# A gated recurrence and a squared-ReLU layer pair: the second token group's second layer wholly in three passes, with six weight differences summed in DRAM by GpSimd's DMAs

## The chip, the cores and the metric

The kernel runs on one core of a Trainium2 chip. The metric is the device time of one execution in microseconds (us). Three runs of the kernel before gave 520.93, 521.38 and 521.76 us; the median is 521.38. One more execution was taken by the hardware profiler and took 521.61 us.

The engines are called as in the profile: PE (TensorE, matrix products), PEld (its weight loads), DVE (VectorE), ACT (ScalarE), POOL (GpSimd) and SP (SyncE, which issues most DMAs). Each engine works through its own instructions in program order and waits on semaphores for the others.

## The reference

```python
def _attn_ref(q, k, v, alpha):          # each (4, 8, 768, 48)
    state = np.zeros((B, H, D, D), dtype=np.float32)
    for t in range(S):
        state = alpha[:, :, t, :, None] * state + np.einsum('bhd,bhe->bhde', k[:, :, t], v[:, :, t])
        y[:, :, t] = np.einsum('bhd,bhde->bhe', q[:, :, t], state)
...
def _moe_ref(x, w_in, w_out):           # x (3072, 384), w_in (384, 2048), w_out (2048, 384)
    h = np.maximum(x @ w_in, 0.0)
    return (h * h @ w_out).astype(np.float32)
```

The recurrence's output, turned to 3072 rows of 384, is x. The weights come in 64-bit floats, which the kernel turns into 32-bit ones itself.

## The kernel before

**Groups and layers.** The sequence is cut in chunks of 128 steps; there are 24 blocks (4 batches by 6 chunks), taken in groups of four: six groups of 512 rows of x. For each group PE does the first layer (16 tiles "h" of 128 hidden units by 512 rows) and the second layer (four sums "o" of 128 rows by 384). While a group's layers run, the recurrence of later blocks is woven in, two blocks at a time ("attention"): its sums of logarithms "cs", transposes "T", scores and state sums "sckv", and products "y".

**Two forms of product.** The weights are held in 8 pieces each (two hidden tiles per piece). A plain product in 32-bit floats shows as two PE records. A product in three passes splits both factors into a near part and a rest, in a faster 32-bit form: near by near, rest by rest, and a third pass with the differences of the two. For the weights the parts are wb (near), wl (rest) and wd (difference); for x they are xa, xl, xd; for the hidden tiles ha, hl, hd (some of the ha and hl lie in other buffers, "hx").

- Group 0: first layer plain; second layer six pieces plain, the last two (6 and 7) in three passes (`k0` = 2).
- Group 1: first layer in three passes; second layer pieces 0 to 3 plain, 4 to 7 in three passes (`k1` = 4).
- Groups 2 to 5: both layers in three passes.

**Making the weights' parts.** `prepare` plans four steps per piece: `cast_w` (ACT, L665, makes wb), `rest_w` (DVE through `combine`, L660, makes wl), `scale_w` (ACT, L679, scales wl, then `keep` stores it to DRAM, L670) and `diff_w` (DVE, L660, makes wd and stores it). wb stays on the chip; wl and wd are loaded again for each group by `pump` (L703), in the order of the list `todo`, as slots come free.

**Splitting the hidden tiles.** `split_h` (ACT, L710, makes ha; DVE, L660, makes hl) and `diff_h` (DVE, L714, makes hd) come once per hidden tile that takes part in three passes. In group 1 before there are 8 such tiles.

**The second layer.** `out_plain` issues plain products and takes the sum out on ACT (L843). `out_x` issues the first two passes tile by tile, and joins the plain part on DVE (L857) or, where there is none, takes the sum out on ACT (L861). `out_y` issues the third passes, piece pairs for each of the four sums, adds on DVE (L660, "osb") and stores. All its products are at L820, those of the first layer in three passes at L737.

**The order of work.** `weave` runs a list of PE units with estimated costs and inserts events (attention steps, weight preparation, splits of x) at planned times, counted in these costs; the planned times stand in the table `AT`. Nothing is reordered afterwards: each engine's order is the order of the calls. `sp` (DVE, L287 and L288) makes "hi" and "lo" of the logarithms for the matmuls of `cs` (L300, L301). `bl` and `br` take one row through DRAM by SP's DMAs (L334, L344, "last<-row") for DVE's `next_state` (L490). In `ga` a marker on GpSimd (L529) waits for PE, and PE's products of `gb` wait for that marker. `align` (L1018) inserts NOPs into PE's instructions at the places and pads of `AT`.

Of the kernel before, what the change touches and what calls it, by code (L numbers as in the profile page):

```python
# [18 lines left out]
AT = {'v_by': (2.5, 3.5, 5.0), 'before': 2.2, 'places': ((4, 203), (16, 188)), 'pads': ((1, 33.0, 218), (2, 0.5, 83), (2, 5.5, 178)), 'evs': 0.65, 'lead': 4, 'post': 3, 'w_first': (45.25, 42.0, 55.95), 'wstep': 1.6, 'w_in_at': 2.5, 'w_late': 0.6, 'w_in_by': 3.4, 'room1': 22, 'room': 25, 's0': 4, 'ahead': 6, 'late': 2, 'xs': 0.2, 'g0': ((1.5, 4, False, True, 28.25), (20.25, 6, True, True), (28.75, 8, True, False)), 'sc0': (2.35, 2.35, 2.35), 'g1': ((5.5, 8, False, 15.5), (15.5, 10, True), (34.5, 12, True)), 'g': ((1.7, 6, True), (15.5, 8, True)), 'g1x': 50.0, 'gx': 48.25, 'g0x': 55.25, 'k0': 2, 'h0': 16, 'k1': 4, 'h1': 3, 'h1by': 2, 'evs0': 0.3, 'tp': 'ADMD', 'tp1': 'ADAD', 'split': 8, 'o0': (44.75, 47.25), 'o1': (), 'o2': (21.75, 27.5, 31.75, 35.0, 41.25, 41.75), 'str1': 22.0, 'ga': 9.5, 'gb': 13.0, 'cv0': 1.5, 'first': 'ln0 warm0 cs0 load0v load2a ei0 load1v eb0 mk0 ln1 fill1 fill1 kT0 cs1 kc0 eb1 mq0 qT0 mq1 ei1 qc0 fill1 mk1 fill1 lt0 sc0 lt1 kT1 kv0 qT1 am0 ln2 weights2 us0 load2q kc1 qc1 cs2 sc1 fill1 am1 load2k ei2 load3a eb2 load4a fill1 kv1 st0 first0 us1 fill1 middle0 ln3 mq2 load3k ya0 qT2 yb0 mk2 fill1 qc2 kT2 cs3 kc2 load3q load2v weights5 sc2 eb3 load3v fill1 sga0 sgb0 fill1 ei3 ev0 mq3 mk3 am2 fill1 late0 qT3 kT3 sgc0 first1 kc3 qc3 middle1 kv2 ha0 sc3 us2 kv3 sga1 ha1 am3 us3 sgb1 load4k ya2 load4q load4v first2 yb2 late0 sgc1 middle2 weights6 ev2 lt3 lt2 st2 ha3 ha2 sgb2 sga2 hb1 sgc2 hb0 hb2 weights1 st1 hb3 st3 weights0'}  # L19
# [6 lines left out]
def kernel(  # L26
# [634 lines left out]

    def cast_w(w, p):
        need(("w", p + (NW if w == "o" else 0)))
        b = here["b", w, p] = wt("wb", FP32R, shapes[w])
        nc.scalar.activation(out=b, in_=whole[w][p], func=AF.Copy, scale=NEAR)  # L665
# [3 lines left out]
    def keep(x, w, p):  # L669
        nc.sync.dma_start(out=kept_parts[x, w, p], in_=words(made[x, w, p]))  # L670
        stored.add((x, w, p))

    def rest_w(w, p):
        l = made["l", w, p] = wt("wl", FP32R, shapes[w])
        combine(((l, whole[w][p], ALU.subtract, here["b", w, p].bitcast(FP32)),))

    def scale_w(w, p):
        l = made["l", w, p]
        nc.scalar.activation(out=l, in_=l.bitcast(FP32), func=AF.Copy, scale=1.0 / E)  # L679
        keep("l", w, p)  # L680

    def diff_w(w, p):
        b, l = here["b", w, p].bitcast(FP32), made["l", w, p].bitcast(FP32)
        d = made["d", w, p] = wt("wd", FP32R, shapes[w])
        cut.add((w, p))
        combine(((d, b, ALU.subtract, l),))
        keep("d", w, p)
        for x in "ld":
            t = made.pop((x, w, p))
            if w == "i" or p >= NW - AT["k0"] or (x == "l" and p >= NW - AT["k1"]):  # L690
                here[x, w, p] = t
        pump()

    def prepare(at, w, p, late=0):
        step = AT["wstep"]
        fs = (cast_w, rest_w, scale_w, diff_w)
        return [(at + i * step + late * (i > 1), f, (w, p)) for i, f in enumerate(fs)]
# [11 lines left out]
    def split_to(a, l, x):  # L709
        nc.scalar.activation(out=a, in_=x, func=AF.Copy, scale=NEAR)  # L710
        combine(((l, x, ALU.subtract, a.bitcast(FP32)),))

    def diff_to(d, a, l):
        nc.vector.scalar_tensor_tensor(  # L714
            out=d, in0=a.bitcast(FP32), scalar=-E, in1=l.bitcast(FP32), op0=ALU.mult, op1=ALU.add
# [66 lines left out]

    def layer_in(g):
        units = []
        for n in range(NJ + 2):
            if n < NJ:
                units.append((1.05, in_x, (n,)))
            if 0 <= n - 2 < NJ:
                units.append((0.53, in_y, (n - 2,)))
            if 0 <= n - AT["post"] < NJ:  # L790
                units.append((0, in_post, (n - AT["post"],)))
            if AT["lead"] <= n < AT["lead"] + AHEAD and (g > 1 or AT["k1"] == NW):
                units += splits_of_h(0, n - AT["lead"])
# [22 lines left out]
    def splits_of_h(first, i):  # L816
        return [(0, split_h, (first + i, i)), (0, diff_h, (first + i,))]
# [18 lines left out]
    def out_plain(p, t, pieces):  # L836
# [3 lines left out]
        for n in (2 * p, 2 * p + 1):  # L840
            of_tile(t, hid[n], w_out[p][:, n % 2], start=n == 0, stop=n == 2 * pieces - 1)
        if p == pieces - 1:
            nc.scalar.activation(out=new_out(t), in_=acc.pop(t)[:, 0:DM], func=AF.Copy)  # L843

    def out_x(n, first):
        p, jj = divmod(n, 2)
        a, l = h_parts.pop(n)
        for t in range(GB):
            if n == first:
                new_sum(t)  # L850
            of_tile(t, a, here["b", "o", p][:, jj], start=n == first)
            of_tile(t, l, here["l", "o", p][:, jj], stop=n == NJ - 1)
            if n == NJ - 1:
                x = acc[t][:, 0:DM]
                if first:
# [25 lines left out]
    def layer_out(g):  # L881
        posts = [(0, in_post, (n,)) for n in range(NJ + 2 - AT["post"], NJ)] if g else []
        plain = NW - AT["k0"] if g == 0 else NW - AT["k1"] if g == 1 else 0
        first = 2 * plain
        units = [(1, out_plain, (p, t, plain)) for p in range(plain) for t in range(GB)]
        if plain:
            for i, x in enumerate(posts):
                units.insert(1 + 2 * i, x)
            posts = []
        if plain == NW:  # L890
            for t in range(GB):
                units.append((0, lambda t: store(g, t, out_tile(t)), (t,)))
            return units
        ahead = AT["ahead"]
        split = [f for i in range(0 if plain else AHEAD, NJ - first) for f in splits_of_h(first, i)]
        if g == 0:
            split = [f for i in range(NJ - first) for f in [(0, split_h, (first + i, 0)), (0, diff_h, (first + i,))]]
        if plain:
            at = AT["h0" if g == 0 else "h1"]
            for i in range(min(AHEAD, len(split) // 2)):  # L900
# [5 lines left out]
        for n in range(first, NJ):  # L906
            units.append((1.08, out_x, (n, first)))
            if posts:
                units.append(posts.pop(0))
            while split and NJ - (len(split) + 1) // 2 <= n + ahead and (  # L910
                split[0][1] is diff_h or split[0][2][1] - AHEAD - MORE <= n - first
            ):
                units += [split.pop(0), split.pop(0)]
        ps = list(range(plain, NW))
        steps = [ps] if g == NG - 1 else [ps[i : i + 2] for i in range(0, len(ps), 2)]
        for pair in steps:
# [28 lines left out]

    def ffn_out(g, t, i):
        per = NJ // NW
        if i == 0:
            acc[t] = ps_ffn.tile([128, GB * C], FP32, tag="att", name="o")
        for j in range(per):  # L950
            nc.tensor.matmul(
                out=acc[t][:, 0:DM],
# [234 lines left out]
```

## Time and profile before

| what | value |
|---|---|
| runs, median (lowest to highest) | 521.38 us (520.93 to 521.76) |
| profiled execution | 521.61 us, of which the traced span is 519.8 us |
| granted PE clock | 1.0 |
| PE busy | 511.1 us (98%) |
| DVE busy | 361.9 us (70%) |
| ACT busy | 316.4 us (61%) |
| POOL busy | 5.4 us (1%) |
| chain that ended last | PE 93%, DVE 3%, DMA 1% |
| largest groups of the chain by line | L820 41%, L737 32%, L930 8% |
| HBM traffic | 84.17 MB read, 17.33 MB written |
| DMA queue of SP | 101.52 MB, 68.6% of the 16 engines' span |

The busy share is an average over stages, so the profile is read by stage: the trace puts the start of group 1's first layer at 126.4 us, of its second layer at 169.0, and of group 2 at 214.8. A row of a group of instructions gives line, engine, operation, out<-in, shapes and count, then busy time and the mean of one in ns, then the idle time of the engine ahead of it and what ended it. Rows in order of time give start, duration and, in brackets, the idle time before. Durations of neighbouring rows of one engine overlap a little, since an instruction starts before the last one's results are all written; the distance of two starts tells what an instruction costs in a full queue. No DMA is issued by POOL in this kernel.

### The profile page before, as it was taken

How to read it: one execution, taken by the hardware profiler on the slowest of the kernel's cores; microseconds unless marked ns; L12 is line 12 of the kernel's file. 1: busy time of each engine (PE TensorE's matmuls, PEld its weight loads, DVE VectorE, ACT ScalarE, POOL GpSimd, SP SyncE). 2: the span in 40 equal slices, each digit the busy share in tenths (PEclk: the TensorE clock that was granted, in tenths of full speed). 3: DMA queues.
4: the chain of work that ended last, by engine and by line, in shares of the span. 5: the costliest groups of instructions: out<-in, count | busy, mean ns of one | idle time of the engine just before them, and what ended most of it. 6: DMA issues, size and time to landing. Idle time of an engine off the chain costs nothing.

```text
span 519.8 us, 13204 instructions
## 1 busy us (share of the span) xinstructions
PE 511.1 (98%) x5350; PEld 421.5 (81%) x5350; DVE 361.9 (70%) x629; ACT 316.4 (61%) x664; POOL 5.4 (1%) x29
## 2 busy tenths in 40 slices
PE   8989999999999999999999999999999999999997
PEld 6775446668887669888899988899988899988997
DVE  3887969998979579757596466696465485363861
ACT  5678893687899566476963266962266863164620
POOL 4000000000000000000000000000000000000000
PEclk9999999999999999999999999999999999999999
DMA  9999686517878496998885796965684534798101
GB/s 182 210 262 262 178 216 172 75 51 240 243 228 200 117 280 161 272 338 234 201 235 156 242 269 185 231 172 162 217 269 124 183 123 153 254 355 295 68 0 62
DMA packets 139324, 102.36 MB, mean 197 GB/s; under 512 B 109808, under 2 KB 112896, under 8 KB 139264
## 3 DMA queue, kind: packets, MB, share of 16 engines
q1 hardware_dynamic: 139264, 101.52, 68.6%
q8 instruction: 43, 0.70, 0.6%
q14 instruction: 17, 0.14, 0.1%
HBM read 84.17 MB, written 17.33 MB: 195 GB/s over the span
## 4 chain that ended last, share of the span: by engine, by line
PE 93%; DVE 3%; DMA 1%; SPq 1%; issue 1%; ACT 0%; DVEq 0%; POOLq 0%
PE o L820 41%; PE h L737 32%; PE h L930 8%; PE y L412 4%; PE T L590 2%; PE sckv L432 2%; PE sckv L460 2%; DVE x L628 1%; DMA a_in<-in_alpha_dram 1%; PE cs L297 1%; SPq L344 1%; DMA last<-row 1%; PE cs L301 1%; PE cs L300 1%; SPq L119 0%
## 5 line engine op out<-in xcount | busy, mean ns | idle before, releaser
L737 PE MATMUL h<-xa,wb 128*128 128x512 f32 x240 | 69.2, 396 | 1.2 <-PE h L737 0.8
L737 PE MATMUL h<-xl,wl 128*128 128x512 f32 x240 | 68.1, 392 | 0.0
L737 PE MATMUL h<-xd,wd 128*128 128x512 f32 x240 | 66.6, 393 | 0.0
L754 ACT ACTIVATE h<-h 128x512 f32<-128x512 f32 x40 | 23.3, 581 | 57.9 <-PE h L737 57.7
L660 DVE TENSOR_TENSOR hid<-h,hid 128x512 f32<-128x512 f32 x40 | 27.5, 688 | 42.1 <-PE h L737 39.3
L628 ACT COPY x<-y 32x256 f32<-32x256 f32 (+2 forms) x132 | 47.2, 365 | 15.7 <-PE y L412 13.2
L820 PE MATMUL o<-wb,ha 128*128 128x384 f32 x160 | 54.2, 339 | 0.0
L820 PE MATMUL o<-wd,hd 128*128 128x384 f32 x304 | 53.7, 334 | 0.0
L820 PE MATMUL o<-w_out,hid 128*128 128x384 f32 x160 | 53.5, 490 | 0.0
L820 PE MATMUL o<-wl,hl 128*128 128x384 f32 x160 | 53.5, 334 | 0.0
L737 PEld LDWEIGHTS h<-xl,wl 128*128 128x128 f32 x240 | 44.9, 188 | 10.6 <-ACT wl L679 0.6
L737 PEld LDWEIGHTS h<-xa,wb 128*128 128x128 f32 x240 | 44.2, 188 | 11.1 <-PE h L737 1.2
L820 PEld LDWEIGHTS o<-wd,hd 128*128 128x128 f32 x304 | 52.8, 188 | 0.0
L737 PEld LDWEIGHTS h<-xd,wd 128*128 128x128 f32 x240 | 44.5, 188 | 9.2 <-ACT hid L752 0.2
L820 PE MATMUL o<-wb,hx 128*128 128x384 f32 x144 | 48.7, 338 | 0.0
L820 PE MATMUL o<-wl,hx 128*128 128x384 f32 x144 | 48.1, 334 | 0.0
L820 PEld LDWEIGHTS o<-w_out,hid 128*128 128x128 f32 x160 | 29.9, 190 | 19.7
L930 PE MATMUL h<-x,w_in 128*128 128x512 f32 (+1 forms) x120 | 43.0, 510 | 1.5 <-DVE s L489 1.2
L710 ACT ACTIVATE ha<-hid 128x512 fp32r<-128x512 f32 x40 | 25.4, 636 | 23.8 <-DVE hx L660 12.9
L752 ACT ACTIVATE hid<-h 128x512 f32<-128x512 f32 x40 | 24.3, 607 | 25.1 <-PE h L737 25.0
L930 PEld LDWEIGHTS h<-x,w_in 128*128 128x128 f32 x120 | 22.5, 190 | 18.6 <-issue 14.9
L660 DVE TENSOR_TENSOR hl<-hid,ha 128x512 fp32r<-128x512 f32 x40 | 27.4, 685 | 10.9 <-ACT ha L710 10.8
(115 smaller groups left out, 883.0 us busy)
## 6 DMA issues: line engine op xcount, KB each, us to landing
wd<-do SPq DMA_DIRECT2D x36, 384.0 KB
wl<-lo SPq DMA_DIRECT2D x34, 384.0 KB
wl<-li SPq DMA_DIRECT2D x32, 384.0 KB
wd<-di SPq DMA_DIRECT2D x32, 384.0 KB
raw<-in_moe_w_in_dram SPq DMA_DIRECT2D x8, 768.0 KB
raw<-in_moe_w_out_dram SPq DMA_DIRECT2D x8, 768.0 KB
v_in<-in_v_dram SPq DMA_DIRECT2D x24, 192.0 KB
out_dram<-osb SPq DMA_DIRECT2D x24, 192.0 KB
```

What stands on the lines that cost most here:

```text
L412: ins = nc.tensor.matmul(out=ys[e][64 * half : 64 * half + D + G * e, m % 2, p // 2, t], lhsT=lhsT, rhs=rhs, start=(half, e) not in seen, ...
L432: nc.tensor.matmul(out=ps[e][HALF[h], 0, p, :], lhsT=ks[rows, p, HALF[h]], rhs=qs[rows, p, HALF[h]], start=True, stop=True, skip_group_che ...
L460: nc.tensor.matmul(out=ps[h][64 * e : 64 * (e + 1), 1, p, G:64], lhsT=tile_of("k", n)[HALF[h], 2 * p + e, :], rhs=tiles["v"][n % NV][HALF[ ...
L590: nc.tensor.transpose(out=ps[h][:, i, p, :], in_=rows[HALF[h], 128 * p : 128 * (p + 1)], identity=ident[HALF[h], HALF[h]],)
L628: copy(out=x[kk][to : to + m, t : t + 2], in_=blk[n]["y"][e][r : r + m, :, p // 2],)
L660: nc.vector.tensor_tensor(out=o, in0=x, in1=z, op=op)
L710: nc.scalar.activation(out=a, in_=x, func=AF.Copy, scale=NEAR)
L737: nc.tensor.matmul(out=acc["h", j], lhsT=here[w, "i", p][:, kk, jj * 128 : (jj + 1) * 128], rhs=x_parts[x][:, kk], start=start and kk == 0 ...
L752: nc.scalar.activation(out=hid[j], in_=x, func=AF.Copy, scale=E)
L754: nc.scalar.activation(out=x, in_=x, func=AF.Copy, scale=1.0 + E)
L820: nc.tensor.matmul(out=acc[t][:, 0:DM], lhsT=lhs[:, t * C : (t + 1) * C], rhs=rhs, start=start, stop=stop, skip_group_check=True,)
L930: nc.tensor.matmul(out=ps, lhsT=w[:, kk, c0 : c0 + 128], rhs=xT[g][kk][:, cols], start=(kk == 0), stop=(kk == KM - 1),)
```

## The change

Group 1's second layer is done in three passes for all 8 pieces, so `out_plain` is left to group 0. To have the parts that were made first at hand, group 1 takes its pieces, in both layers, in the order 6, 7, 0, 1, ... 5 (`pieces`, `tiles_of`); the preparation of pieces follows that order. Three hidden tiles are split during group 1's first layer, as it already was in the later groups, and the planned times of the w_out pieces (`o2`) are 20 to 35 in place of 21.75 to 41.75.

For the six w_out pieces 0 to 5 (`added`) DVE makes no wd. GpSimd stores wb to the DRAM tile of the difference, then a second DMA of GpSimd adds wl to it there; wl of these pieces is stored by GpSimd too. To make the difference a sum, near parts of weights, x and hidden tiles get the opposite sign (`scale=-NEAR`), rests are made by adding, and the hidden tiles' difference has its sign turned, so products keep theirs. `landed` lets the sums be loaded again 10 units after a piece's first step. In group 1 all eight wd of w_out are loaded from DRAM (four before); wl of pieces 0 to 5 stays on the chip from its making. Options no longer used are taken out, and the places and pads of `align` are others: two pads in group 1 (one before) and none in group 2 (two before).

```diff
-... 'places': ((4, 203), (16, 188)), 'pads': ((1, 33.0, 218), (2, 0.5, 83), (2, 5.5, 178)), ...
+... 'places': ((4, 207), (16, 203)), 'pads': ((1, 9.0, 84), (1, 33.0, 50)), ... 'landed': 10.0, ...
-... 'k1': 4, 'h1': 3, ... 'o1': (), 'o2': (21.75, 27.5, 31.75, 35.0, 41.25, 41.75), ...
+... 'o2': (20.0, 23.0, 26.0, 29.0, 32.0, 35.0), ...
...
+    def added(w, p):
+        return w == "o" and p < NW - AT["k0"]
...
     def cast_w(w, p):
...
-        nc.scalar.activation(out=b, in_=whole[w][p], func=AF.Copy, scale=NEAR)
+        nc.scalar.activation(out=b, in_=whole[w][p], func=AF.Copy, scale=-NEAR)
+        if added(w, p):
+            nc.gpsimd.dma_start(out=kept_parts["d", w, p], in_=words(b))
...
     def keep(x, w, p):
-        nc.sync.dma_start(out=kept_parts[x, w, p], in_=words(made[x, w, p]))
+        by = nc.gpsimd if added(w, p) else nc.sync
+        by.dma_start(out=kept_parts[x, w, p], in_=words(made[x, w, p]))
...
     def scale_w(w, p):
         l = made["l", w, p]
         nc.scalar.activation(out=l, in_=l.bitcast(FP32), func=AF.Copy, scale=1.0 / E)
+        if added(w, p):
+            nc.gpsimd.dma_start(out=kept_parts["d", w, p], in_=words(l), accum_op=ALU.add)
         keep("l", w, p)
...
     def diff_w(w, p):
...
+        if added(w, p):
+            return
...
+    def landed(w, p):
+        if added(w, p):
+            stored.add(("d", w, p))
+            pump()
...
+    def pieces(g):
+        last = [*range(NW - AT["k0"], NW)]
+        return last if g == 0 else last + [*range(NW - AT["k0"])] if g == 1 else [*range(NW)]
+
+    def tiles_of(g):
+        return [2 * p + i for p in pieces(g) for i in range(2)]
...
-            if AT["lead"] <= n < AT["lead"] + AHEAD and (g > 1 or AT["k1"] == NW):
-                units += splits_of_h(0, n - AT["lead"])
+            if AT["lead"] <= n < AT["lead"] + AHEAD:
+                units += splits_of_h(js, n - AT["lead"])
...
-        plain = NW - AT["k0"] if g == 0 else NW - AT["k1"] if g == 1 else 0
-        first = 2 * plain
+        plain = NW - len(ps)
...
-            events.append((at0 + AT["str1"], stream_out, (AT["k1"], "d")))
+            events.append((at0 + AT["str1"], stream_out, (order, "d")))
```

## The prediction

> **What bounds the kernel now.** I read the share of busy time first (PE 98%), then the chain that ended last (PE 93%, and in the stretch of the change nothing but PE rows), then each engine's busy time by stage, and last the rows of DVE, PE and the DMA queue in order of time. The second group's first layer runs from 126.4 to 169.0 us, its second from 169.0 to 214.8. Busy time in these two; columns PE, weight load, DVE, ACT, POOL, clock, DMA share, GB/s:
>
> ```profile
> 126.40:169.00 42.60, 42.60 (x506) 34.11 (x504) 37.54 (x68) 37.74 (x77) 0.00 (x0) 1.00 0.76 206
> 169.00:214.80 45.80, 45.80 (x551) 36.01 (x550) 36.23 (x65) 28.04 (x63) 0.00 (x0) 1.00 0.73 203
> ```
>
> PE never stands still, at full clock, so PE work taken out shortens the kernel if no other engine becomes late. But DVE, which the change loads, is busy 73.8 of these 88.4 us. The chain in order of time (start, us, what) prices PE's work:
>
> ```profile
> 169.03 5.36 PE o L820 x16
> ...
> 175.93 10.52 PE o L820 x32
> ...
> 187.15 5.16 PE o L820 x16
> ...
> 266.43 29.32 PE o L820 x168
> ```
>
> The first three rows are the 32 plain multiplications (two records each): 21.04 us, 0.657 each. The last is passes of the three-pass form in the next group, 0.1745 each; the 96 passes of this stage take 17.26 in the same list, 0.180 each.
>
> The rows of DVE and PE in order of time show the place that decides. "lo" (L288) is the last DVE result that the cumulative sums "cs" (L300, L301) of the third attention pair need:
>
> ```profile
> 185.71 0.56 DVE L288 TENSOR_TENSOR lo<-a_in,hi 128x384 fp32r<-128x384 f32 x1
> ```
> ```profile
> 175.86 10.59 PE L820 MATMUL o<-w_out,hid 128*128 128x384 f32 x32
> 185.99 0.63 PE L300 MATMUL cs<-hi,causal_r 128*128 128x384 f32 x1
> 186.47 0.33 PE L301 MATMUL cs<-lo,causal_r 128*128 128x384 f32 x1
> 186.63 0.34 PE L300 MATMUL cs<-hi,causal_r 128*128 128x384 f32 x1
> 186.81 0.34 PE L301 MATMUL cs<-lo,causal_r 128*128 128x384 f32 x1
> ```
>
> DVE delivers that lo at 186.27; the matmul that reads it starts at 186.81. So DVE is half a microsecond ahead here, and PE, which works in order, stops for all that DVE is later.
>
> **The change, step by step**, on the clock of the profiled execution before (521.61 us, its span 519.8).
>
> 1. *PE loses work.* 32 plain multiplications become 96 passes of 0.1745 to 0.180: 21.04 - 16.75 or - 17.26, a gain of 3.8 to 4.3. I take **-4.1**.
>
> 2. *DVE gets work ahead of that lo.* I counted its instructions in program order from the first "xd" of this group (127.60) to that lo: 86 before, 108 after. The 22 more are 11 pairs hl/hd or hx/hd, the splits of hidden tiles (3 pairs stood ahead of it, now 14). Two more wl and two fewer wd cancel (950 and 951 ns). What a pair costs, back to back:
>
> ```profile
> 194.12 0.69 DVE L660 TENSOR_TENSOR hx<-hid,hx 128x512 fp32r<-128x512 f32 x1 [2.46 <-ACT hx L710]
> ...
> 199.58 1.82 DVE L660 TENSOR_TENSOR wl<-w_out,wb 128x768 fp32r<-128x768 f32 x2
> ```
>
> Four pairs fill 194.12 to 199.58, 1.365 each: 11 make **15.0 us**. Room for them are DVE's gaps in that stretch: 0.45, 0.29, 0.35, 2.46, 0.67, 0.33, 2.82, 0.87, 1.38, together 9.6. If all are filled, lo is 5.4 late. They will not all be: the first three (1.1) wait for ACT results that come no earlier. The 2.82 waits for a DMA:
>
> ```profile
> 171.97 0.36 DVE L490 TENSOR_TENSOR s<-s,last 128x192 f32<-128x192 f32 x1 [2.82 <-DMA last<-row]
> ```
>
> In the SP queue these row loads (166.25 to 170.41) stand behind a store of a "wd" that DVE makes at 162.08. Three added pairs (4.1) precede that wd and can fill 2.46 + 0.35 of gaps, so the wd, the loads and their landing move by 1.2 or so; DVE's own arrival moves by 1.2 to 1.5 (4.1 and one wl more, against gaps of 3.8). The wait stays near 2.9 (an estimate; bounds 0 and 3.5). Filled gaps are then 9.6 - 1.1 - 2.9 = 5.6, and lo is 9.4 late, at 195.7. PE comes to the place with 88 passes (15.4 to 15.8) in place of 24 plain ones (15.88), 0.3 earlier; less the half microsecond of lead, PE stops for **+9.2** (bounds 5.0 with every gap filled, 10.5). Earlier stops, at the hx and wl that single tiles need, are parts of it: the same queue is late for them by less.
>
> 3. *What is late next.* The sixth wl leaves DVE two pairs and itself after lo (2.7 + 0.87) and ACT's scaling 0.85 later, 4.4 in all; PE needs it after the cs (0.7) and 24 passes (4.2). A tie: nothing added, up to 0.5 kept. The x splits and osb sums stand where DVE has 10 us with little to do.
>
> 4. *ACT* makes 8 more "ha" (0.636 each by L710's group), three of them in the first layer, where it is busy 37.7 of 42.6 us. That may hold PE by up to 1.9, but PE would then only come later to a cs whose lo is later still. Nothing; 1.9 if step 2 were gone. Four osb sums (L857, 0.55) leave DVE, behind the place.
>
> 5. *GpSimd* gets 18 DMAs of 384 KB: six stores of wb, six that add wl to them in DRAM, six stores of wl. None is in the trace of before; SP's do<-wd, issued at 173.83, has landed when the load that waits for it starts at 176.46, so 2.6 us. For one that adds I take 5.2 (it also reads), bounds 2.6 and 7.8. Behind a DMA that waits in GpSimd's queue stands its marker at L529, for which PE's "gb" products wait. The first such (PE's y at 174.4) has one adding DMA ahead, whose wl ACT has scaled at 167.4 before, 169 after: 5 us of cover. The sixth wl is added from 200.1 to 205.3, loaded as wd by 208 to 211; PE's last out_y wants it about 217. Nothing, but 3 if a queue is held up.
>
> 6. *SP* loses 12 stores and gets 4 loads more; the next group's li loads stand behind the load of the sixth sum, at 206 in place of 207.9, with PE 5 us later. Nothing. The new order of the first layer's pieces changes no count.
>
> 7. *Pads.* Two align markers leave the third group. The first costs PE time now (rows of NOPs; PE's gap in brackets):
>
> ```profile
> L1018 PEldq NOP  x26: 13/13/13, 215.0 to 216.9; - x26
> ```
> ```profile
> 216.97 0.93 PE L737 MATMUL h<-xa,wb 128*128 128x512 f32 x3 [0.81 <-PE h L737]
> ```
>
> **-0.8** (bounds -1.2, with the 0.38 that PE waits for DVE at 241.8, and 0, if code placed otherwise costs as much). Two new pads in the second group lie where PE waits anyway.
>
> Sum: 521.61 - 4.1 + 9.2 - 0.8 = 525.9. The median of the runs, 521.38, is 0.2 below the profiled execution: **525.7**.
>
> **A rule against the change.** The cast rows (L287, 354 ns for 128x384, where L288 takes 558) show DVE in a faster mode for casts; six of them lie in the second group.
> The Trainium skill, SBUF - State Buffer, section "Who interferes with whom", says that DVE in a two-port mode and GpSimd lock each other out of a shared port pair for a whole instruction, whoever comes first, and that GpSimd needs it to write DMA descriptors. The trace agrees on the faster cast; no run here shows the lock. By that page a cast ahead of the late lo could stand behind a descriptor job; with about 1 us for one, an estimate from the first-byte latency in the Trainium skill, DMA: Bandwidth & Descriptors, section "Specifications", two such casts would make the sum 527.7.
>
> **Rivals.**
> - *Gaps filled* (20%): the row loads land early enough and DVE fills nearly all gaps; PE stops for 5.0 to 7.5. Then 521.6 - 4.1 + 6 - 0.8, 522.5 on the runs' scale (521 to 524). For it: gap sizes. Against it: the row loads' place behind a wd.
> - *Faster* (10%): DVE runs its pairs as it runs single instructions, 0.60 apart (hid at 134.79, the next at 135.39): 11 pairs are 13.2, and with every gap filled PE stops for 3.2, which gives 519.7. The point: PE gains if lo is under 4.9 late, and with no stop at all it is 516.5. Against it: hd reads the hl just ahead of it, and all four rows of pairs above are 1.365.
> - *GpSimd late* (13%): stores and sums meet DMA engines that are full (share 1.05 and more from 181 to 186 and 191 to 196), the marker or SP's waiting load comes after its cover, and 3 more are lost: 528 to 529.5. For it: last<-row took SP 4.16 us to issue.
> - The forecast, 524 to 528: 57%. That it does not do what it says is excluded by the program order: PE has 96 passes more and no plain ones there.
>
> About 0.2% (1.0 us) is what a measurement tells from no change. Faster than that: the faster rival, 10%. Within: half of "gaps filled" and a little, 12%. Slower: 78%. The range, 520.5 to 529.5, leaves out most of the faster rival and the end of the GpSimd one.
>
> **What would show it.** Step 1: 192 passes at 0.175 to 0.18 and no plain rows in that stage. Step 2: an idle row of PE ahead of cs put down to DVE lo (L288), or spread over hx, hl and wl just ahead, 9 us together, and DVE busy nearly without gaps from 172 to 200. Step 5: no PE wait on POOL. Step 7: no gap at the start of the third group. I am wrong if PE's waits in the second group are under 5 us, or if they name ACT, POOL or a DMA.

## The result, and the profile after

Four runs of the changed kernel took 534.88 to 536.65 us, median 535.68; four runs of the kernel before, beside them, 519.99 to 521.76, median 521.15. The ratio is 1.028 (1.026 to 1.031): slower by 14.5 us, where the prediction had said slower by 4.3 and at most 529.5 us. The profiled execution took 534.88 us, its span is 533.1.

Where the time came in can be read from five points on PE's clock, each as us from the start of the span. Columns: first "h" of the second group, first "o" of its second layer, last "cs" of the third attention pair, first "h" of the third group, end.

| kernel | first layer | second layer | last cs | third group | end |
|---|---|---|---|---|---|
| before | 126.3 | 169.0 | 186.8 | 214.6 | 519.8 |
| after | 126.9 | 172.5 | 201.5 | 227.1 | 533.1 |
| after is late by | 0.6 | 3.5 | 14.7 | 12.5 | 13.3 |

So 2.9 us arise in the first layer, 9.0 in the second, hardly any later. Busy time in these two layers of the kernel after (columns as for the kernel before):

```profile
126.90:172.50 45.60, 43.27 (x506) 34.72 (x505) 41.82 (x74) 39.67 (x80) 2.68 (x4) 1.00 0.72 200
172.50:227.10 54.60, 46.91 (x583) 43.07 (x580) 31.58 (x59) 29.50 (x67) 9.36 (x14) 0.94 0.93 247
```

PE, never idle before, is idle 2.3 and 7.7 us; in the first layer DVE is now busy 41.8 of 45.6; in the second the granted clock is 0.94 and the DMA share 0.93 (0.73 before). PE's waits in these layers (who waits, for whom: sum, times, longest):

```profile
PE cs L300 <- DVE hi L287: 3.9, 1, 3.9
PE o L844 <- DVE hl L660: 1.9, 2, 1.6
PE T L590 <- DVE q_in L316: 1.8, 1, 1.8
PE o L844 <- DVE hx L660: 1.2, 1, 1.2
PE o L844 <- issue: 0.5, 1, 0.5
PE h L753 <- ACT wl L687: 0.5, 1, 0.5
```

The place is the one that was forecast: cs waits for DVE, and hl and hx ahead of it do too. The 0.5 without a name ("issue") is the new pad: the last of its no-operations starts at 188.38, the pass behind it at 188.45. But DVE has a wait of its own. Its rows in order of time, around the state's update, with the last "hid" ahead of it that waits for PE, and around the lo that decides (L288):

```profile
168.75 0.69 DVE L660 TENSOR_TENSOR hid<-h,hid 128x512 f32<-128x512 f32 x1 [0.93 <-PE h L753]
...
172.81 0.36 DVE L489 TENSOR_TENSOR s<-sckv,us 128x192 f32<-128x192 f32 x1
179.22 0.36 DVE L490 TENSOR_TENSOR s<-s,last 128x192 f32<-128x192 f32 x1 [6.05 <-DMA last<-row]
179.50 0.68 DVE L660 TENSOR_TENSOR hx<-hid,hx 128x512 fp32r<-128x512 f32 x1
...
200.91 0.56 DVE L288 TENSOR_TENSOR lo<-a_in,hi 128x384 fp32r<-128x384 f32 x1
```

DVE comes to "s" 4.0 us later than before (172.81 against 168.79); 3.6 of it stand at that hid already, for which PE's h comes late (168.75 against 165.16). Then it stands 6.05 us for a row from DRAM (2.82 before), and has hardly a gap from there to lo. lo is done at 201.47, 15.2 late: 4.0 by arrival, 3.2 by the longer wait, 8.0 by work behind the wait that found no gap. The row's load stands in SyncE's queue like this, after and before:

```profile
168.52 1.63 SPq L119 DMA_DIRECT2D q_in<-in_q_dram  x2
170.25 3.59 SPq L344 DMA_DIRECT2D last<-row  x4
173.94 1.39 SPq L119 DMA_DIRECT2D k_in<-in_k_dram  x1
```
```profile
164.50 1.66 SPq L119 DMA_DIRECT2D q_in<-in_q_dram  x2
166.25 4.16 SPq L344 DMA_DIRECT2D last<-row  x4
170.51 0.39 SPq L670 DMA_DIRECT2D lo<-wl  x1
```

The order is the same. But DVE goes on 1.6 us after the last issue before (170.41 to 171.97), and 5.4 us after it now (173.84 to 179.22). GpSimd's own transfers take long to land (size, median us from issue to landing):

```profile
do<-wb POOLq DMA_DIRECT2D x6, 384.0 KB, 4.8
do<-wl POOLq DMA_DIRECT2D x6, 384.0 KB, 6.2
lo<-wl POOLq DMA_DIRECT2D x6, 384.0 KB, 6.6
```

PE's rows at the place, and the stretches around them (us, then PE, weight load, DVE, ACT, POOL, clock, DMA share, GB/s):

```profile
188.45 0.41 PE L844 MATMUL o<-wb,ha 128*128 128x384 f32 x1 [0.53 <-issue]
190.50 0.41 PE L844 MATMUL o<-wl,hl 128*128 128x384 f32 x1 [1.64 <-DVE hl L660]
...
200.16 0.42 PE L300 MATMUL cs<-hi,causal_r 128*128 128x384 f32 x1 [3.86 <-DVE hi L287]
...
201.52 0.69 PE L301 MATMUL cs<-lo,causal_r 128*128 128x384 f32 x1
202.01 0.52 PE L844 MATMUL o<-wb,hx 128*128 128x384 f32 x1
202.33 0.52 PE L844 MATMUL o<-wl,hx 128*128 128x384 f32 x1
...
205.16 0.35 PE L844 MATMUL o<-wl,hx 128*128 128x384 f32 x1
205.34 0.34 PE L844 MATMUL o<-wb,hx 128*128 128x384 f32 x1
```
```profile
186.40:191.40 5.00, 2.80 (x12) 2.29 (x13) 4.81 (x10) 3.21 (x8) 1.44 (x2) 0.96 0.75 173
191.40:196.40 5.00, 4.90 (x20) 4.58 (x19) 4.76 (x8) 4.98 (x10) 1.99 (x3) 0.70 0.90 231
196.40:201.40 5.00, 1.16 (x3) 0.56 (x3) 4.72 (x10) 2.63 (x5) 2.00 (x3) 0.99 0.97 235
201.40:206.40 5.00, 4.94 (x21) 4.88 (x21) 4.93 (x10) 2.33 (x5) 0.23 (x1) 0.67 0.98 230
```

Behind two of PE's stops the passes start 0.32 us apart (202.01 to 202.33) in place of 0.18 (205.16 to 205.34), and the granted clock of those stretches is 0.70 and 0.67. One stop is that of cs, 3.86 us; the other is the pair of 0.53 and 1.64 above. Ten passes at 191.1 to 194.3 and eight at 202.0 to 204.6 are slow, 18 times 0.14, 2.5 us; the four cs take 1.85 us to the next pass in place of 1.16. A stop can cost PE more than its own length. What is lost ahead of cs is no loss of its own, since PE waits there for lo in any case; behind cs it is 0.7 and eight passes, 1.1 us.

In the first layer PE now stands at a turn of q and k:

```profile
145.33 0.46 PE L590 MATMUL T<-ident,k_in 64*128 64x64 f32 x8
147.61 0.46 PE L590 MATMUL T<-ident,q_in 64*128 64x64 f32 x8 [1.82 <-DVE q_in L316]
```

Ahead of that q_in (DVE's row at 147.00) DVE makes three pairs hl/hd of the early splits, which the kernel before does not have there.

### The profile page after: what moved, and what is told of

Read it like the earlier page. It is cut to its first block, busy times and chain, and to the rows that moved or that the text cites. A ratio compares the mean times of both kernels' runs of the same rounds, so it can differ in the third digit from the quotient of the medians.

```text
span 533.1 us, 13257 instructions
## 1 busy us (share of the span) xinstructions
PE 515.0 (97%) x5382; PEld 430.1 (81%) x5382; DVE 364.7 (68%) x635; ACT 320.4 (60%) x672; POOL 17.4 (3%) x47
## 4 chain that ended last, share of the span: by engine, by line
PE 83%; DVE 7%; DMA 4%; ACT 3%; SPq 1%; issue 1%; POOL 0%; DVEq 0%; ACTq 0%; POOLq 0%
PE o L844 35%; PE h L753 27%; PE h L944 7%; PE y L412 3%; PE T L590 2%; PE sckv L432 2%; DMA last<-row 2%; ACT x L628 2%; PE sckv L460 1%; DMA k_in<-in_k_dram 1%; DMA raw<-in_moe_w_in_dram 1%; SPq L344 1%; DVE hd L730 1%; PE cs L297 1%; PE zeros L398 1%
## 5 line engine op out<-in xcount | busy, mean ns | idle before, releaser
L844 PE MATMUL o<-wl,hl 128*128 128x384 f32 x176 | 60.2, 342 | 1.9 <-DVE hl L660 1.9
L844 PE MATMUL o<-wb,ha 128*128 128x384 f32 x176 | 60.7, 345 | 0.5 <-issue 0.5
L844 PE MATMUL o<-wd,hd 128*128 128x384 f32 x336 | 59.8, 335 | 0.0
L844 PEld LDWEIGHTS o<-wd,hd 128*128 128x128 f32 x336 | 58.2, 188 | 0.1
L844 PE MATMUL o<-wl,hx 128*128 128x384 f32 x160 | 54.4, 340 | 1.2 <-DVE hx L660 1.2
L844 PE MATMUL o<-wb,hx 128*128 128x384 f32 x160 | 54.7, 342 | 0.0
L726 ACT ACTIVATE ha<-hid 128x512 fp32r<-128x512 f32 x44 | 27.9, 634 | 27.8 <-DVE hx L660 17.1
L944 PE MATMUL h<-x,w_in 128*128 128x512 f32 (+1 forms) x120 | 42.9, 510 | 1.6 <-DVE s L489 1.4
L768 ACT ACTIVATE hid<-h 128x512 f32<-128x512 f32 x40 | 24.2, 606 | 25.2 <-PE h L753 25.1
L660 DVE TENSOR_TENSOR hl<-hid,ha 128x512 fp32r<-128x512 f32 x44 | 30.2, 685 | 10.6 <-ACT ha L726 10.5
L844 PEld LDWEIGHTS o<-wl,hl 128*128 128x128 f32 x176 | 33.8, 192 | 2.7 <-ACT x L628 1.9
L844 PEld LDWEIGHTS o<-wb,ha 128*128 128x128 f32 x176 | 33.8, 192 | 1.3 <-issue 0.8
```

The source lines that it names most:

```text
L660: nc.vector.tensor_tensor(out=o, in0=x, in1=z, op=op)
L726: nc.scalar.activation(out=a, in_=x, func=AF.Copy, scale=-NEAR)
L768: nc.scalar.activation(out=hid[j], in_=x, func=AF.Copy, scale=E)
L844: nc.tensor.matmul(out=acc[t][:, 0:DM], lhsT=lhs[:, t * C : (t + 1) * C], rhs=rhs, start=start, stop=stop, skip_group_check=True,)
L944: nc.tensor.matmul(out=ps, lhsT=w[:, kk, c0 : c0 + 128], rhs=xT[g][kk][:, cols], start=(kk == 0), stop=(kk == KM - 1),)
```

## The experiments

Three theories were put up at first. **A:** the amount of DVE's work in its order, with its wait for the row, is the loss. **B:** GpSimd's DMAs crowd out the others. **C:** DVE's backlog is only handed on, so that taking away one part lets another take its place. All but the last two runs are single executions; the changed kernel's own runs scatter by 1.8 us, so times are read to about that, and the five points of the trace (us late against the kernel before) more finely:

| run | first layer | second layer | last cs | third group | end | time, us |
|---|---|---|---|---|---|---|
| after | 0.6 | 3.5 | 14.7 | 12.5 | 13.3 | 535.68 |
| sums on VectorE | 0.0 | 4.4 | 14.0 | 13.0 | 14.0 | 535.56 |
| plain stores by SyncE | 0.6 | 4.8 | 12.9 | 10.7 | 13.5 | 535.11 |
| splits at 11 to 13 | 0.6 | 3.1 | 11.9 | 10.2 | 12.2 | 533.78 |
| splits at 8 to 10 | 0.4 | 5.9 | 17.3 | 14.5 | 15.1 | 536.71 |
| row by TensorE | 0.4 | 5.2 | 9.4 | 8.0 | 14.6 | 536.19 |
| the same, sums on VectorE | 0.9 | 7.3 | 14.8 | 13.4 | 16.3 | 537.90 |
| lo sooner | 1.1 | 5.3 | 12.5 | 13.7 | 14.9 | 536.46 |
| rows sooner (timed) | 1.4 | 5.8 | 10.4 | 8.4 | 9.9 | 530.72 |
| rows, splits, lo | 0.2 | 5.6 | 7.1 | 8.3 | 9.8 | 531.43 |
| before, with the sums | 0.5 | 0.5 | 1.5 | 7.9 | 6.9 | 528.42 |
| before, six pieces | -0.1 | 0.1 | 8.6 | 14.7 | 14.9 | 536.52 |

One part of these points is not made by the edits. The granted clock in the traces is either 1.0 or 0.5, and ahead of the end of the span a stretch at 0.5 lasts 3.4 us or a multiple of it. The same stop in the first layer (0.5 for ACT's wl, then 1.8 for q_in) stands in ten runs: after, 1, 2, 5, 6, 9, 10, 13, 15 and 18. In eight of them a stretch at 0.5 begins during it or within 2.1 us behind it; in the kernel after and in run 9 none does. Here is what comes behind that stop in the kernel after, and in run 18:

```profile
148.94 0.96 PE L753 MATMUL h<-xd,wd 128*128 128x512 f32 x3
```
```profile
149.74 1.65 PE L753 MATMUL h<-xd,wd 128*128 128x512 f32 x3
151.18 1.48 PE L753 MATMUL h<-xa,wb 128*128 128x512 f32 x3
```

In runs 1, 6, 15 and 18 (3.4 us at 0.5) the first layer is 1.3 to 1.5 us longer by it than in the kernel after, in run 13 (6.8 us) 2.4. Run 18 has another such stretch from 33.6 to 37.0 us, ahead of the first point. So differences of that size in the column of the second layer are not read as the work of an edit.

**1. Sums on VectorE.** The changed kernel without any DMA of GpSimd; `diff_w` makes every wd on DVE.

```diff
-            nc.gpsimd.dma_start(out=kept_parts["d", w, p], in_=words(b))
...
-        by = nc.gpsimd if added(w, p) else nc.sync
-        by.dma_start(out=kept_parts[x, w, p], in_=words(made[x, w, p]))
+        nc.sync.dma_start(out=kept_parts[x, w, p], in_=words(made[x, w, p]))
...
-            nc.gpsimd.dma_start(out=kept_parts["d", w, p], in_=words(l), accum_op=ALU.add)
...
-        if added(w, p):
-            return
```

> The changed kernel with the six differences made by DVE again and all their stores issued by SP; GpSimd issues no DMA, the rest is as changed. Base: the changed kernel's profiled execution, 534.9 us. Theory A (the amount of DVE work in order, with its wait of 6.05 us for the row DMA): DVE gets six wd more at 0.87, some 3.5 of them ahead of the late cs, and loses at most the 3.8 by which the row DMA landed more slowly than before: 533 to 537. Rival B (GpSimd's DMAs crowd out the others, and that is the loss): the row lands within 2 us of its issue, the wait of DVE falls below 3 us, and the time falls to 531 or less.

535.56 us. DVE's wait for the row at this place is short now, and cs waits for hi 6.0 us all the same:

```profile
175.92 0.36 DVE L490 TENSOR_TENSOR s<-s,last 128x192 f32<-128x192 f32 x1 [1.16 <-DMA last<-row]
```

Without GpSimd's transfers the DMA share at 173 to 176 us is 0.39 in place of 1.10, and DVE goes on 1.6 us after the row's last issue (174.33), as in the kernel before. The differences on DVE, about 0.9 us each, three of them between the row and lo, eat up most of the gain, and half clock in the first layer the rest. So A gives the time, but B is no mere rival: with the transfers gone the row is not late.

**2. Row by TensorE.** `br` calls `lt` for blocks 10 and 11, which turns the row with 16 small products each in place of the trip through DRAM.

```diff
+    BY_PE = (10, 11)
...
-        if n // B < NCH - 1:
+        if n in BY_PE:
+            lt(n)
+        elif n // B < NCH - 1:
```

> The changed kernel, but the rows of blocks 10 and 11 go from ACT's result to their place by eight small PE products per block and two ACT copies, as the first four blocks do it, in place of two stores and four loads through DRAM. Theory A with the row wait as a part of its own: DVE's gap of 6.05 ahead of the state product disappears, everything behind it in DVE's queue comes 5 to 6 us earlier, PE's stop at cs falls with it, and the clock falls less: 527 to 530. Rival C (the amount of DVE work alone; the gap would be filled by other waits): 533 to 535.

542.07 us, which neither theory gave. PE stood 12.9 us with nothing named, and in that time its sequencer went through no-operations of the pad:

```profile
L1018 PEldq NOP  x218: 13/13/13, 188.3 to 204.3; - x109
```

The pad fills up to a place in a block of 256 instructions. The edit adds 64 instructions ahead of it (32 products and their weight loads), so the pad grew from 26 to 218: a fault of the experiment, not of the kernel. The same befell runs 5, 7 and 8; runs 9 to 12 repeat the four with the places moved on.

**3. Splits at tiles 11 to 13** in place of 4 to 6 of the first layer.

```diff
-            if AT["lead"] <= n < AT["lead"] + AHEAD:
+            lead = 11 if g == 1 else AT["lead"]
+            if lead <= n < lead + AHEAD:
```

> The changed kernel, but the three hidden tiles that are split during group 1's first layer are split seven tiles later in it. Theory A: PE's stops in the first layer (0.50 for wl, 1.82 for q_in at the transposes) go, 2.3 to 2.8 us; DVE's total is the same, so the rest stays: 531.5 to 533.5. Rival C (the backlog is only moved, and what the first layer gains is lost at the cs): 534 to 536.

533.78 us: just above A's range, under C's. The wait of T at 147.6 is gone, but one of 1.94 us stands at the next turn, at 163.9. The wait had been moved, not removed. DVE's wait for the row is 3.43 us there, so the 1.9 us that this run gains may be the row's; they were not separated.

**4. Before, with the sums.** The kernel before with GpSimd's 18 DMAs and the signs turned; four pieces stay plain.

```diff
+        by = nc.gpsimd if added(w, p) else nc.sync
...
+            nc.gpsimd.dma_start(out=kept_parts["d", w, p], in_=words(l), accum_op=ALU.add)
```

> The kernel before with nothing but the DRAM sums: the six w_out pieces 0 to 5 have their differences added in DRAM by GpSimd and their wb and wl stored by GpSimd, signs turned accordingly; group 1 keeps four plain pieces and the order of pieces. Base: before, 521.2 us. Theory A: DVE loses six wd that nothing waited for, and GpSimd's DMAs are hidden: 520 to 522.5. Rival B (GpSimd's DMAs cost by themselves): 524 or more, with PE waiting behind a DMA or behind GpSimd's marker.

528.42 us against 521.07 beside it: the sums alone cost 7.3 us, and relieve DVE of six differences at that. Up to the last cs it is only 1.5 late. Then come 6 us: DVE's wl is to be written into a slot from which GpSimd's store has not yet been read, and PE waits for the us that stands behind it. The clock is at 0.5 from 209.0 to 215.8, which makes up the rest.

```profile
207.02 0.96 DVE L660 TENSOR_TENSOR wl<-w_out,wb 128x768 fp32r<-128x768 f32 x1 [4.91 <-DMA lo<-wl]
```
```profile
210.45 0.86 PE L432 MATMUL sckv<-qs,ks 48*64 48x64 f32 x10 [3.55 <-DVE us L473]
```

**5. Row by TensorE, sums on VectorE** (edits 1 and 2 together).

> The changed kernel with the six differences taken by VectorE, all stores by SyncE (no DMA of GpSimd is left), and with the last rows of blocks 10 and 11 turned by TensorE instead of fetched through DRAM. It takes away both things that can make VectorE stand before the third pair's cs: the row's DMA (5.4 us in the run with differences on VectorE) and the traffic of GpSimd. If the amount of VectorE's work alone decides, the eleven added pairs and the differences still stand ahead of lo, less the wait of about 5 us: 529 to 532 us, with one wait of TensorE for hi or lo of 1 to 3 us. If the waits of VectorE were only time in which it would have had nothing else to do, the time stays at 534 to 536.5. If TensorE stops again for 10 us or more with nothing named, as in the run with the row by TensorE, that stop belongs to the row by TensorE and not to GpSimd's DMAs, and the time is 538 or more.

544.0 us: the pad again, 218 no-operations. (The 5.4 us that this expectation names for run 1 was its longest wait for a row, at 220.7 us; at the place it was 1.16.)

**6. Plain stores by SyncE,** only the adding DMAs by GpSimd.

```diff
-            nc.gpsimd.dma_start(out=kept_parts["d", w, p], in_=words(b))
+            nc.sync.dma_start(out=kept_parts["d", w, p], in_=words(b))
...
-        by = nc.gpsimd if added(w, p) else nc.sync
-        by.dma_start(out=kept_parts[x, w, p], in_=words(made[x, w, p]))
+        nc.sync.dma_start(out=kept_parts[x, w, p], in_=words(made[x, w, p]))
```

> The changed kernel with the twelve plain stores (do<-wb, lo<-wl) issued by SyncE and only the six adding ones by GpSimd. The bytes are the same. If the row lands late because of the bytes that stand on the DMA engines ahead of it, the wait for it stays at 5 to 7 us or grows, since SyncE now issues the stores ahead of it in its own order: 534 to 537 us. If it is late because of GpSimd's own queue, the wait falls to 3 us and the time to 529 to 532.

535.11 us, a split verdict: the time is that of the case in which the bytes count, the wait for the row (3.35 us) is near that of the other. The DMA share at 170 to 176 us is 1.12 (1.15 with GpSimd's stores). The time is that of the changed kernel within the scatter, whichever engine issues the plain stores; half clock in the first layer is 1.3 us of it.

**7. Before, six pieces** (`k1` = 6, `o2` of the changed kernel).

> The kernel before with k1 = 6 in place of 4, and the preparations of the second weights at the changed kernel's times: six of eight pieces of the second group's second layer in three passes, two still by plain multiplications, all differences on VectorE, no DMA of GpSimd. Half the dose of the change in VectorE's pairs. If the stop of TensorE grows in proportion to the pairs, 526 to 529 us. If VectorE's gaps take in the first half and the second half is what costs, 520 to 523.5. If even half fills VectorE's queue as the whole does, 531 or more.

554.31 us, with a pad of 251 no-operations: spoiled.

**8. Before, sums and row by TensorE.**

> The kernel before with the sums in DRAM and GpSimd's stores (528.4 us as it was run), and with the last rows of blocks 10 and 11 turned by TensorE. In that run two waits of VectorE stood on the chain: 6.1 us for the row's DMA and 5.6 us for a slot from which GpSimd's lo<-wl had not yet been read. If the row is the price of GpSimd's DMAs, the time comes back to 521 to 524. If the slots are, it stays at 526 to 529.

539.19 us, with a pad of 218: spoiled.

**9. Row by TensorE, pad mended.**

```diff
-... 'places': ((4, 207), (16, 203)), 'pads': ((1, 9.0, 84), (1, 33.0, 50)), ...
+... 'places': ((4, 207), (16, 11)), 'pads': ((1, 9.0, 84), (1, 33.0, 114)), ...
```

> The run with the row by TensorE once more, with the place of the pad at 33 us moved on by 64. In that run TensorE stood 12.9 us with nothing named because the pad (no-operations up to a place in a block of 256 instructions) had grown from 26 to 218 of them: the 32 added multiplications and their loads of weights had moved it past its place. With 26 again, what is left is the row. If VectorE's wait of 6.05 us for the row's DMA is the part of its delay that was under-estimated, lo comes 5 to 6 us sooner and the time is 527 to 530 us. If the work that stands behind the wait is held by something else (ACT's ha, the second weights), it is 533 to 536.

536.19 us, so the time spoke against it; the trace does not. The last cs comes 5.3 us sooner than in the changed kernel and the third group starts 4.5 sooner, as expected. It is lost again in the fourth group, which takes 84.0 us in place of 79.4: PE stands there 2.0 us in y and 0.5 in o with nothing named, and behind the first the clock is at 0.5 from 327.4 to 330.8. The code behind the pad lies 64 instructions further on in its blocks than in the changed kernel.

**10. The same with sums on VectorE.**

> The run with differences on VectorE, stores by SyncE and the row by TensorE once more, with that pad moved on by 64 as well (it had 218 no-operations there too). No DMA of GpSimd and no wait for a row: VectorE's added work alone, eleven pairs and the differences. If that alone is the price: 528 to 532 us and a wait of TensorE for hi or lo of 1 to 4 us. If hardly anything is left without the waits: 520 to 524.

537.9 us, cs waits for hi 6.1: a miss. From the second layer's start to the last cs it takes 25.3 us, run 9 takes 22.0, the changed kernel 29.0. The differences on DVE cost 3.3 us of the 7 that the row's wait is worth.

**11. Before, six pieces, pads mended.**

> The run with six pieces (the kernel before with k1 = 6) once more; there the pad at the start of the third group had grown to 251 no-operations (18.5 us). Its place and the two behind it are moved on by 31. What is left is the first half of the added pairs with all differences on VectorE and no DMA of GpSimd; the wait for cs of 5.4 us was there already, ahead of the pad. If that wait is the price, 530 to 536 us. If the pad's stop had also brought about much else, 524 to 529.

536.52 us, just above the range: half the pieces, and the whole loss. At the last cs it is 8.6 late, some 60% of the changed kernel's; then 6 more are lost, of them 3.4 in a stop of PE without a name (last section), which half clock follows from 212.2 to 219.0. The dose is not clean, since the preparations come earlier too.

**12. Before, sums and row by TensorE, pads mended.**

> The kernel before with sums in DRAM, GpSimd's stores and the row by TensorE once more, with all pads behind the added multiplications moved on by 64 (the first had 218 no-operations). If the late row is the price of GpSimd's DMAs (528.4 us with the row through DRAM), 521 to 524. If the slots held by GpSimd's stores are, 526 to 529.

538.09 us, above both. The wait for the slot is still there (4.56 us), so the late row is not all that the sums cost in the kernel before. PE has two stops without a name, 2.2 us at 171 and 2.9 us at 326, so nothing is read from the time.

**13. Rows sooner.** Here TensorE's instructions are untouched: only the row of blocks 10 and 11 goes out and comes back earlier in SyncE's queue.

```diff
+    ROWS = {"bl": 3.2, "br": 5.2}
...
+                if n0 == 10 and f[:2] in ROWS:
+                    w = t + ROWS[f[:2]]
```

> The changed kernel with only the order of SyncE's transfers altered for the pair of blocks 10 and 11: the row goes out at 3.2 and comes back at 5.2 us of the pair's plan in place of 4.0 and 6.5, ahead of v, li, k, di and q. TensorE's instructions are the same, in the same places. If VectorE's wait of 6.05 us for the row is what makes its delay longer than forecast, the wait falls to 2 us or less, the last cs comes 3 to 5 us sooner and the time is 529.5 to 532.5. If the time stays at 534 to 536.5, what stands behind the row fills the time anyway.

531.85 us, and timed in rounds (run 18) 530.72 (530.18 to 531.55), 5.0 under the changed kernel. DVE's wait is gone:

```profile
174.85 0.36 DVE L489 TENSOR_TENSOR s<-sckv,us 128x192 f32<-128x192 f32 x1
175.25 0.36 DVE L490 TENSOR_TENSOR s<-s,last 128x192 f32<-128x192 f32 x1
175.52 0.69 DVE L660 TENSOR_TENSOR hx<-hid,hx 128x512 fp32r<-128x512 f32 x1
```

PE's waits in the two layers of run 18 are those at the early splits and at cs; hl and hx are not among them any more:

```profile
PE cs L300 <- DVE hi L287: 3.5, 1, 3.5
PE T L590 <- DVE q_in L316: 1.8, 1, 1.8
PE h L753 <- ACT wl L687: 0.5, 1, 0.5
```

**14. Splits at tiles 8 to 10** (edit 3 with 8).

> The changed kernel with the three early splits of the second group at tiles 8 to 10 of its first layer in place of 4 to 6: between the two turns of q and k of that layer, where they delay neither. In the run with them at 11 to 13 the wait of 1.8 us had only gone to the second turn. If the splits are what made the first 3.5 us of the loss (the second layer starts at 172.5 in place of 169.0), it now starts at 169.5 to 171 and the time is 531.5 to 533.5. If VectorE's later standing swallows that, 534 to 536.5.

536.71 us, and the second layer starts later still, 5.9 late. T does not wait; sckv, h and cs wait in its place (0.9, 1.1, 1.3 and 0.8 us). In the three places tried, the first layer with the early splits takes 45.2 to 48.2 us. In runs 4, 11 and 17 and in the kernel before, which have none there, it takes 42.7 to 42.9; in run 12, which has none either, 44.0 and then a stop of 2.2 without a name. No run takes the early splits out of the changed kernel.

**15. lo sooner.** The steps `ln` and `sp` of the third pair 8 us earlier.

```diff
+                if n0 == 12 and f[:2] in ("ln", "sp"):
+                    w -= 8.0
```

> The changed kernel with the logarithms of the third pair and their hi and lo 8 us sooner in the order (ahead of some nine pairs of hl and hd); TensorE's instructions are the same. If the wait is only one of order, lo for cs being last, the wait for cs goes and no other of its size comes: 526 to 530. If VectorE is full from 179 to 207, so that whatever is last is late, the wait for cs goes and TensorE waits for hl or hx by as much: 532 to 536.

536.46 us. cs waits for nothing, and PE's waits in the second layer are now these:

```profile
PE o L844 <- ACT wl L687: 3.8, 3, 1.8
PE o L844 <- DVE hl L660: 3.2, 2, 2.0
PE o L844 <- DVE hx L660: 1.0, 1, 1.0
PE o L844 <- DMA wd<-do: 0.9, 1, 0.9
```

ACT's wl is late because ACT waits for DVE's wl (1.79 us at 201.5, 1.82 at 206.4). DVE is busy 25.2 of the 28 us from 179 to 207. It is the amount, not the order: what is last in DVE's queue is late, whatever it is.

**16. Rows, splits and lo together** (edits 13, 14, 15).

> All three together: rows sooner, early splits between the turns, lo sooner. If the three parts of the loss add up (splits 2 to 3, row 3 to 5, order 0 to 4), 524 to 529 us. If each only passes its time on to the next, 531 or more. Faster than the kernel before (521) is expected by neither.

531.43 us: no better than the rows alone, so the parts do not add up (C, for the splits and the order). The clock stays at 1.0 up to the end; the longest stop in the two layers is 1.9 us.

**17. Before, rows sooner** (edit 13 in the kernel before).

> The kernel before with only the row of blocks 10 and 11 sent and fetched sooner, as in the run that took 531.85 us. There VectorE stood 2.82 us for the row, in the second group. If VectorE has room in the kernel before, so that this wait costs TensorE nothing, the time is that of the kernel before, within 0.2% (520 to 522); if it stood on the path there too, 518 to 519.5.

521.67 us; ratio 1.0003 (0.9988 to 1.0018). DVE's wait of 2.82 us is gone and it gains nothing: where DVE has room, the same wait is free.

**18. Rows sooner, in rounds.**

> The changed kernel with the rows sooner, once more and in rounds, since it is the largest single part found: 531 to 533 us again, 3 to 4.5 us under the changed kernel's 535.68. If it is nothing but scatter between runs (534.88 to 536.65), 534 or more in some of them.

530.72 us, ratio to the kernel before 1.017 (1.015 to 1.019). This is the best of the changed kernels, and still slower than the kernel before; no version faster than that was found.

## Why the prediction was wrong

The sign, the place and the mechanism were right: DVE's lo for the third pair's cs comes late, and PE stops there and ahead of it. The size was 4.3 us for 14.5. Two terms failed: the wait for the row (step 2), which the DMAs that step 5 put at nothing made longer, and the early splits (step 4, put at nothing). What a stop does to PE's clock was left out. By steps, against the trace:

1. *PE loses work, -4.1.* Held: at full clock the passes start 0.17 to 0.18 us apart.
2. *DVE's added pairs.* Their number and price held (14 pairs ahead of lo, starts 1.32 to 1.40 apart). The term that was mis-sized is **the wait for the row, "near 2.9 (an estimate; bounds 0 and 3.5)"**: it was 6.05, and rows sooner gains 5.0 us. The estimate only moved the issues in SyncE's queue. It took the time to land from the kernel before, where the share of the DMA engines falls to 0.36 at 169 to 172; with GpSimd's stores it stays at 1.1. DVE's arrival there, forecast 1.2 to 1.5 late, was 4.0 late (step 4). Behind the row the forecast's 9.4 leaves about 7.9 for the work that finds no gap: measured 8.0, so that part held, and the sign "DVE busy nearly without gaps from 172 to 200" holds from 179 on only. PE's waits in the second layer add up to 7.5 us, inside the bounds for the stop and even under the forecast 9.2: PE itself comes 3.5 late, and part of its time ahead of cs goes into half clock. Left out was what a stop does behind cs: 0.7 us in the cs and 1.1 in slow passes.
3. *The sixth wl, a tie.* Nothing in the waits of the kernel after speaks against it; it was not tested by itself. With lo sooner, ACT's wl becomes PE's longest wait (3.8).
4. *The three early splits, nothing.* **Wrong, 2.9 us.** It was argued that PE would only come later to a cs whose lo is later still. But DVE waits for PE too: the hid at 168.75 waits 0.93 us for PE's h, which comes 3.6 late (0.6 of it from the first group), and the "s" behind it is 4.0 late. A delay of PE ahead of DVE's own inputs does not run beside DVE's delay; it is added to it. That the splits make PE's delay is read from the rows of T and q_in, and run 3 moved the wait with them.
5. *GpSimd's DMAs, nothing.* **Wrong.** The landing of the adding one was sized well (6.2, estimate 5.2, bounds 2.6 and 7.8), the plain stores took 4.8 and 6.6 where SP's took 2.6, and no PE wait in these layers names POOL. But they delay the row (1.16 us of wait without them, 6.05 with them). In the kernel before they cost 7.3 us in a single run, whose trace shows a slot held by a store, PE's stop behind it and half clock. The rival "GpSimd late" had the resource right, the victim wrong (the marker or SyncE's load, where it was the row), and the price low (3 us, where the row gave 5.0). The "rule against the change" does not show: the casts at L287 take 353 ns on average (354 before), and DVE's one wait from 172 to 202 is that for the row.
6. *SyncE, nothing.* The order held; its row was late for step 5's reason.
7. *Pads, -0.8.* The gap at the start of the third group is gone, yet that group is 0.7 us longer. Its first six passes take 2.7 us (227.13 to 229.87) in place of 1.4, with DVE's xl on the chain there, and PE waits 0.80 for DVE's hid at 255.0 where it waited 0.38. The forecast's own bound (0) was the better value.

Added up on the span, 13.3 us late against a forecast of 4.3. lo is 15.2 late in place of 9.4: 2.6 more by DVE's arrival (0.6 of it from the first group, not traced in full) and 3.2 by the row. Behind it come 1.8 in the cs and the slow passes, and 1.5 in the third group (0.7 for -0.8). That makes 9.1; the measured excess is 9.0.

Undoing parts does not give these back one by one: the row gives 5.0, moving the splits and the order nothing. The remaining 9 us are read as DVE's amount in a stretch where it has no room. Run 15 supports this, but no run takes the amount alone away, and in run 16 5.4 of the 9.8 still lost arise in the first layer, where PE waits for ACT as well as for DVE.

Left open: what the early splits cost altogether, and how many bytes of GpSimd's the row could bear.

## What to carry to other kernels

An engine that gets close to full turns its free waits into paid ones: the same wait for a row cost nothing where DVE had room (run 17) and 5 us where it had none (run 18), so price each wait of the loaded engine again, and with the new traffic on the DMA engines. Moving work off an engine by DMA was not free here, with transfers of 384 KB: they delayed a small one for which the engine waits, and held a slot that it writes next. Before two runs are compared, look where each runs at half clock: the same stop brought it in one run and not in another. And an edit that adds instructions moves every block of code behind it; look at the pads and at stops without a name before you read the time.

## What the hardware showed that was not expected

- *The clock after a stop.* Each stretch at half clock ahead of the span's end lasts 3.4 us or a multiple (6.8, 10.2, 13.7, 17.1), with passes 0.32 us apart in place of 0.18. The Trainium skill, TensorE: Matmul & The Clock Gate, section "Part 1: The HAM clock gate", has the clock halved after an idle window of some 3.4 us and given back after as long a busy one; the trace agrees with the halving and with the length of the slow stretches. No unbroken stop of that length was needed: one of 1.64 (with 0.53 just ahead) brought it in the kernel after, one of 1.82 in eight of ten runs, and run 16 with stops up to 1.9 kept the clock at 1.0.
- *Stops of PE without a name.* In run 11 PE stands 3.4 us in a burst of small products:

```profile
213.66 0.48 PE L412 MATMUL y<-am,v_in 64*64 64x64 f32 x5 [3.42 <-issue]
```

  The trace has a packet of 16 KB on the instruction queue at 211.31 to 212.20, in the middle of the stop; in run 12 one runs from 170.19 to 171.58, and PE, which had stood since 170.8, goes on at 173.00. The 1.96 us in run 9 (PE goes on at 326.54, a packet ends at 325.19) and a second stop in run 12 (329.05 and 327.72) look the same: in all four PE goes on 1.3 to 1.5 us after the packet's end. It looks as if the next block of code came late; no experiment isolated it. The Trainium skill, Runtime: NRT & Kernel Launch, section "Instruction fetch mechanics", calls this refill mostly hidden; in these three runs it would not be.
- *No-operations.* In run 2, 218 of them took 16.0 us of PE's sequencer, 0.074 each, with the products behind them waiting.
